# A decode kernel on one core: the last 96 rows of w_out loaded into 24 lanes by transfers of six lanes, new ring places for the last unit's keys, halves in the last projection and in the final copy

## The chip, the cores and the metric

The kernel runs on one core of one Trainium2 chip. The metric is the device time of one execution in microseconds (us), of which the median over several runs is compared. The core has five engines with instruction streams of their own: TensorE (PE, matrix products; its weight loads are listed as PEld), VectorE (DVE), ScalarE (ACT), GpSimd (POOL) and SyncE (SP), and 16 DMA engines that move data between device memory and the on-chip memory of 128 lanes (partitions). Matmul results go to PSUM.

## The reference

One decode step for 4 sequences of one token, D = 640: `out = x + attention(ln(x)) + gmlp(ln(x))`. Cut to what matters:

```python
q = (xn @ wq).reshape(4, 1, 32, 128).transpose(0, 2, 1, 3)
p = softmax(einsum('bhqd,bhkd->bhqk', q, k_cache) * 128 ** -0.5)   # 4 x 32 heads, 4096 keys each
o = einsum('bhqk,bhkd->bhqd', p, v_cache)
attention = o.reshape(4, 1, 4096) @ wo                             # wo: 4096 x 640
z = gelu(xn @ w_in)                                                # w_in: 640 x 1728
z1, z2 = z[..., :864], layernorm(z[..., 864:])
g = w_sp * z2 + b_sp                                               # one token: w_sp is 1 x 1
gmlp = (z1 * g) @ w_out                                            # w_out: 864 x 640
```

Everything is bfloat16; the key and value caches are 134 MB each and are read once.

## The kernel before, in words

Work is cut into 16 units (`NU`): four groups of eight heads times four sequences. A unit's keys are 8 MB and its values 8 MB. Keys lie in a ring of seven places of 2 MB each (`RING`), four places to a unit; values lie in one buffer, `v_all`. `k_at[u]` says which places a unit's four quarters take, `k_order[u]` in which order they are worked on. Even units take places 3 to 6, odd ones 0 to 3; the last three units have entries of their own. Place 4 also takes a group's rows of wo (`WO_AT`), and places 0 to 3 the last unit's values (`VE_AT`), for which `v_all` comes too late.

The main loop goes over 64 steps `n`, one quarter of a unit's keys each. In a step DVE multiplies the quarter by the query in place (`product`, L490), adds the two halves of each row (`fold_half`, L496), PE adds up the rest by eight matmuls with the identity (`sums`, L505), and DVE finishes the row sums one step later (`row_sums`, L518). At a unit's first step the scores of the unit before become weights (`head_max`, `exps`, `by_head`); a few steps later `weighted` (L575) multiplies them with the values. `turns` says at which step that happens. After a group's last unit, `group_turn` and `group_proj` (L636) multiply by wo and add into `out_ps`, the PSUM tile in which all parts of the output are summed: columns 0 to 319 on partitions 0 to 3, columns 320 to 639 on partitions 32 to 35.

The gMLP is a generator, `gmlp`, whose stages are run in steps 0 to 2. It cuts the 864 rows of w_out in `NFF` = 6 blocks of 128 and one of `FT` = 96. For each block and each half of w_in there are five weight loads and matmuls of four columns (L358), then small DVE and ACT steps on tiles with `NFC` = 7 blocks (L366 to L450), and at the end two matmuls for each block into `out_ps` (L454). The weights wq, w_in and the last 96 rows of w_out (`w_end_sb`, one row to a lane) lie in `v_all` until then; so unit 0's values can be loaded only behind the gMLP.

All large loads are issued by SP, in the order of the list `loads`. `pump` goes through the list at each step and stops at the first entry whose places are still `busy`; in the engine's own stream each transfer then waits for what it really needs. The last entries are two halves of unit 15's values (the second in four pieces of 64, 32, 16 and 16 columns of 256 bytes a lane) and the last group's wo in five transfers: heads 0-1, 2-3, 4-5, 6 and 7. The end of the kernel is those heads' matmuls, one copy of `out_ps` by ACT (L758) and two stores, one from ACT's queue and one from SP's.

Of the kernel before, what the change touches and what calls it, by code (L numbers as in the profile page):

```python
# [17 lines left out]
def kernel(  # L18
# [14 lines left out]
    nc = tc.nc  # L33
    P = nc.NUM_PARTITIONS
    Bsz, Sq, D = A_x.shape
    _, H, S, Dh = A_k_cache.shape
    HD = A_wq.shape[1]
    F = B_w_in.shape[1]
    Fh = F // 2
    DC = D // P  # L40
# [8 lines left out]
    HT = 8  # L49
# [3 lines left out]
    NU = HG * Bsz  # L53
# [6 lines left out]
    QW = HC * Dh  # L60
    RING = 2 * NK - 1
    NFF = Fh // P
    NFC = NFF + 1
    FT = Fh - NFF * P
    NOH = D // 2
    CB = 4
    NG = NR // CB
# [25 lines left out]
    v_all = places.tile([P, NK * QW], BF16, name="v_all")  # L93
# [3 lines left out]
    w_in_sb = v_all[:, DC * HD : DC * (HD + F)].rearrange("p (c n) -> p c n", c=DC)  # L97
    w_out_sb = p_m[:].rearrange("p n g c h -> p (n g c h)")[:, 0 : NFF * D].rearrange(
        "p (k n) -> p k n", k=NFF
    )  # L100
    w_end_sb = v_all[:, DC * (HD + F) : DC * (HD + F) + D]
    nc.sync.dma_start(out=wq_sb, in_=A_wq.rearrange("(p c) n -> p c n", c=DC))

    wsp_bf = const.tile([1, 1], BF16)
# [4 lines left out]
    def load_w():  # L109
        nc.sync.dma_start(out=w_in_sb, in_=B_w_in.rearrange("(p c) n -> p c n", c=DC))  # L110
        nc.sync.dma_start(
            out=w_out_sb, in_=B_w_out[0 : NFF * P].rearrange("(p k) n -> p k n", k=NFF)
        )
        nc.sync.dma_start(out=w_end_sb[:FT], in_=B_w_out[NFF * P : Fh])

    def run_of(cache, u):
        hg, b = divmod(u, Bsz)
# [8 lines left out]
    k_at, k_order = {}, {}  # L126
    for u in range(NU):
        k_at[u] = [r if u % 2 else NK - 1 + r for r in range(NK)]
        k_order[u] = [NK - 1, 0, 1, 2] if u % 2 else [0, 1, 2, 3]
    k_order[NU - 3] = [0, 1, 2, 3]  # L130
    k_at[NU - 2], k_order[NU - 2] = [5, 6, 0, 1], [0, 1, 2, 3]
    k_at[NU - 1], k_order[NU - 1] = [2, 3, 5, 6], [0, 1, 2, 3]
    VE_AT, WO_AT = (0, 2), 4

    def k_load(u, r0=0, r1=NK):
        at = k_at[u][r0:r1]

        def go():
            nc.sync.dma_start(
                out=ring[:, at[0] : at[0] + r1 - r0, :],  # L140
                in_=run_of(A_k_cache, u)[:, r0 * QW : r1 * QW].rearrange("p (r w) -> p r w", w=QW),
            )

        return go, at
# [22 lines left out]
    def wo_load(hg):  # L167
        return (lambda: load_wo(hg)), [WO_AT]

    loads = [k_load(0, 0, 2), (load_w, []), k_load(0, 2, 4), k_load(1)]  # L170
    for u in range(NU - 4):
        loads += [v_load(u), k_load(u + 2)]
        if u % Bsz == Bsz - 1:
# [24 lines left out]
    def load_wo(hg):  # L198
        rows = A_wo[hg * HT * Dh : (hg + 1) * HT * Dh]
        if hg == HG - 1:  # L200
            by_head = rows.rearrange("(h p) n -> p h n", p=P)
            for h0, h1 in ((0, 2), (2, 4), (4, 6), (6, 7), (7, 8)):
                nc.sync.dma_start(out=wo_sb[:, h0:h1, :], in_=by_head[:, h0:h1, :])
            return
        nc.sync.dma_start(
            out=wo_sb.rearrange("p (e j) n -> p e j n", e=PAR),
            in_=rows.rearrange("(e p j) n -> p e j n", e=PAR, j=JR),
        )
# [7 lines left out]
    for e in range(PAR):  # L216
        nc.gpsimd.tensor_copy(
            out=of_row[:, e, :, :, e, :],
# [131 lines left out]
    def gmlp():  # L350
        zz, gw, gt, gz = (gm[n] for n in ("zz", "gw", "gt", "gz"))
        zT = ps_pv.tile([P, 2, NFC, Bsz], FP32, tag="pv", name="zT")
        for t in range(2):
            f1 = t * Fh + NFF * P
            w_t = w_in_sb[:, :, t * Fh : f1].rearrange("p c (f k) -> p c k f", k=NFF)
            for k in range(NFC):
                for c in range(DC):
                    nc.tensor.matmul(  # L358
                        out=zT[: P if k < NFF else FT, t, k, :],
                        lhsT=w_t[:, c, k, :] if k < NFF else w_in_sb[:, c, f1 : f1 + FT],  # L360
                        rhs=xnT[:, c, 0:Bsz],
                        start=(c == 0),
                        stop=(c == DC - 1),
                    )
        yield
        nc.vector.tensor_copy(out=zz[:, :, 0:NFF, :], in_=zT[:, :, 0:NFF, :])  # L366
        nc.vector.tensor_copy(out=zz[:FT, :, NFF, :], in_=zT[:FT, :, NFF, :])
        nc.vector.tensor_tensor(out=gw[:], in0=zz[:], in1=zz[:], op=ALU.mult)
        nc.vector.tensor_scalar(
            out=gw[:], in0=gw[:], scalar1=0.044715, scalar2=1.0, op0=ALU.mult, op1=ALU.add  # L370
        )
        nc.vector.tensor_tensor(out=gw[:], in0=gw[:], in1=zz[:], op=ALU.mult)
        nc.scalar.activation(
            out=gt[:], in_=gw[:], func=ACT.Tanh, scale=math.sqrt(2.0 / math.pi)
        )
        yield
        nc.vector.tensor_scalar(
            out=gt[:], in0=gt[:], scalar1=1.0, scalar2=0.5, op0=ALU.add, op1=ALU.mult
        )
        nc.vector.tensor_tensor(out=gz[:, 0:2], in0=zz[:], in1=gt[:], op=ALU.mult)  # L380
        sq = gz[:, 2, :, :]
        nc.vector.tensor_tensor(out=sq, in0=gz[:, 1, :, :], in1=gz[:, 1, :, :], op=ALU.mult)

        s_ps = ps_m.tile([1, 2, NFC, Bsz], FP32, tag="m", name="ln_ps")
        nc.tensor.matmul(
            out=s_ps[:], lhsT=ones_sq[:, 0:1], rhs=gz[:, 1:3], start=True, stop=True
        )
        yield
        st, ac = gm["st"], gm["ac"]
        mean_t = st[:, 0:Bsz]  # L390
        ex2_t = st[:, Bsz : 2 * Bsz]
        var_t = st[:, 2 * Bsz : 3 * Bsz]
        rst_t = st[:, 3 * Bsz : 4 * Bsz]
        tmp_t = st[:, 4 * Bsz : 5 * Bsz]
        nc.vector.tensor_reduce(
            out=st[:, 0 : 2 * Bsz].rearrange("o (s b) -> o s b", s=2),
            in_=s_ps[:].rearrange("o s k b -> o s b k"),
            axis=AX.X,
            op=ALU.add,
        )  # L400
        nc.vector.tensor_scalar(
            out=st[:, 0 : 2 * Bsz],
            in0=st[:, 0 : 2 * Bsz],
            scalar1=1.0 / float(Fh),
            scalar2=None,
            op0=ALU.mult,
        )
        nc.vector.tensor_tensor(out=tmp_t, in0=mean_t, in1=mean_t, op=ALU.mult)
        nc.vector.tensor_tensor(out=var_t, in0=ex2_t, in1=tmp_t, op=ALU.subtract)
        nc.scalar.activation(  # L410
            out=rst_t, in_=var_t, func=ACT.Sqrt, bias=eps_tile[:1], scale=1.0
        )
        wsp_t = work.tile([1, 1], FP32, name="wsp_t")
        nc.vector.tensor_copy(out=wsp_t[:], in_=wsp_bf[:])
        bsp_t = work.tile([1, 1], FP32, name="bsp_t")
        nc.vector.tensor_copy(out=bsp_t[:], in_=bsp_bf[:])
        yield
        nc.vector.reciprocal(out=rst_t, in_=rst_t)
        nc.vector.tensor_scalar(
            out=ac[:, 0:Bsz], in0=rst_t, scalar1=wsp_t[:, 0:1], scalar2=None, op0=ALU.mult  # L420
        )
        nc.vector.tensor_tensor(out=tmp_t, in0=ac[:, 0:Bsz], in1=mean_t, op=ALU.mult)
        nc.vector.tensor_scalar(
            out=ac[:, Bsz : 2 * Bsz],
            in0=tmp_t,
            scalar1=-1.0,
            scalar2=bsp_t[:, 0:1],
            op0=ALU.mult,
            op1=ALU.add,
        )  # L430
        ac_ps = ps_m.tile([P, 2 * Bsz], FP32, tag="m", name="ac_ps")
        nc.tensor.matmul(
            out=ac_ps[:], lhsT=ones_sq[0:1, :], rhs=ac[:], start=True, stop=True
        )
        ac_sb = work.tile([P, 2 * Bsz], FP32, name="ac_sb")
        nc.scalar.copy(out=ac_sb[:], in_=ac_ps[:])
        yield
        nc.vector.tensor_tensor(
            out=sq,
            in0=gz[:, 1, :, :],  # L440
            in1=ac_sb[:, None, 0:Bsz].to_broadcast([P, NFC, Bsz]),
            op=ALU.mult,
        )
        nc.vector.tensor_tensor(
            out=sq,
            in0=sq,
            in1=ac_sb[:, None, Bsz : 2 * Bsz].to_broadcast([P, NFC, Bsz]),
            op=ALU.add,
        )
        nc.vector.tensor_tensor(out=gm["yT"][:], in0=gz[:, 0, :, :], in1=sq, op=ALU.mult)  # L450
        for k in range(NFC):
            w = P if k < NFF else FT
            for half in range(2):
                nc.tensor.matmul(  # L454
                    out=out_sum(half),
                    lhsT=gm["yT"][:w, k, :],
                    rhs=(w_out_sb[:, k] if k < NFF else w_end_sb[:FT])[
                        :, half * NOH : (half + 1) * NOH
                    ],
                    start=False,  # L460
                    stop=False,
                )
        yield
# [206 lines left out]
    with tc.manual_schedule(engines={E.PE, E.DVE, E.Activation, E.SP}):  # L670
# [84 lines left out]

        res = work.tile([P, NOH], BF16, name="res")
        out_v = out.flatten_outer_dims()
        nc.scalar.copy(out=res[0 : OG + Bsz], in_=out_ps[0 : OG + Bsz])  # L758
        nc.scalar.dma_start(out=out_v[:, 0:NOH], in_=res[0:Bsz])
        nc.sync.dma_start(out=out_v[:, NOH:D], in_=res[OG : OG + Bsz])  # L760

# [29 lines left out]
```

## Time and profile before

| | before |
|---|---|
| median of 3 runs | 662.24 us (662.23 to 663.67) |
| the profiled execution: time, span | 662.98 us, 661.2 us |
| mean granted TensorE clock | 0.687 |
| busy: PE, DVE, ACT | 305.8 us, 522.3 us, 29.8 us |
| DMA: moved, mean rate | 282.54 MB, 427 GB/s |
| q1 (loads from SP), share of 16 engines' span | 99.0% |
| first keys landed, first `product` | 25.9 us, 26.02 us |
| unit 0's values issued | 56.08 us |
| unit 15's first keys issued | 572.2 us |
| last wo transfer issued, landed | 649.6 us, 657.8 us |
| final copy, first store | 658.35 us (0.42 us long), 658.8 us |

The profile is one execution, taken by the hardware profiler. "Span" is the time from its first to its last instruction; the execution's own time has 1.78 us more around it. A row of the timeline gives start, duration, engine, line, operation, output and inputs; in brackets stands how long the engine was idle before and what it waited for. SPq is SP's queue: an entry there is the issue of a transfer, not the transfer.

### The profile page before, as it was taken

The page shows a single profiled execution, that of the slowest core. Times are in us where ns is not written, and L with a number is a line of the kernel's source. Part 1 is how long each engine was busy: PE and PEld are TensorE (multiplying, and loading weights), DVE is VectorE, ACT ScalarE, POOL GpSimd, SP SyncE. Part 2 cuts the span into 40 slices and gives each one's busy share as a digit, 9 for nine tenths or more (in the row PEclk, how much of TensorE's full clock was granted, in tenths as well). Part 3 has the DMA queues.
Part 4 walks back from the last instruction along what each step waited for, and adds up shares of the span by engine and source line. Part 5 has one row for each costly group of instructions (what it writes and reads, how often), then busy time and mean ns, then how long its engine had stood idle before and what let it go on. Part 6 is the DMA issues. An engine that isn't in the chain of part 4 may idle for free.

```text
span 661.2 us, 4618 instructions
## 1 busy us (share of the span) xinstructions
PE 305.8 (46%) x1999; PEld 133.8 (20%) x1999; DVE 522.3 (79%) x325; ACT 29.8 (5%) x73; POOL 2.6 (0%) x12
## 2 busy tenths in 40 slices
PE   0265363526427452362536336263462544737357
PEld 0032121212103221120222212121120221213124
DVE  2578977959598794969959697695969969999950
ACT  0020000000000000000000000000000000000000
POOL 1000000000000000000000000000000000000000
PEclk9666586765857676685867878666685867876575
DMA  9999999999999999999999999999999999999996
GB/s 377 424 459 408 437 441 440 433 444 428 413 444 436 441 424 428 441 428 440 437 437 421 425 444 437 432 432 437 424 437 444 428 430 427 413 437 425 460 399 277
DMA packets 8272, 282.54 MB, mean 427 GB/s; under 512 B 848, under 2 KB 1980, under 8 KB 3132
## 3 DMA queue, kind: packets, MB, share of 16 engines
q1 hardware_dynamic: 8232, 282.24, 99.0%
q8 instruction: 15, 0.25, 0.1%
q14 instruction: 5, 0.04, 0.0%
q10 hardware_dynamic: 20, 0.01, 0.0%
HBM read 282.24 MB, written 0.01 MB: 427 GB/s over the span
## 4 chain that ended last, share of the span: by engine, by line
DMA 64%; DVE 26%; PE 9%; issue 1%; ACT 0%; SPq 0%; DVEq 0%
DMA k_ring<-in_A_k_cache_dram 57%; DVE k_ring L490 14%; PE s_ps L505 7%; DVE k_ring L496 7%; DMA v_all<-in_A_v_cache_dram 4%; DMA k_ring<-in_A_wo_dram 3%; DVE s_sb L518 2%; DVE m L527 1%; PE pv L575 1%; DVE p_m L551 1%; PE out_ps L636 1%; DVE mt L529 0%; DVE mt L532 0%; DVE nm L534 0%; DVE o_n L618 0%
## 5 line engine op out<-in xcount | busy, mean ns | idle before, releaser
L490 DVE TENSOR_TENSOR k_ring<-k_ring,qbc 128x8192 bf16<-128x8192 bf16 x64 | 282.8, 4419 | 91.6 <-DMA k_ring<-in_A_k_cache_dram 91.6
L505 PE MATMUL s_ps<-k_ring,ident 128*128 128x512 bf16 x512 | 199.2, 559 | 320.8 <-DVE k_ring L496 320.6
L505 PEld LDWEIGHTS <-ident 128*128 128x128 bf16 x512 | 65.4, 129 | 434.6 <-issue 385.8
L496 DVE TENSOR_TENSOR k_ring<-k_ring 128x4096 bf16<-128x4096 bf16 x64 | 146.1, 2283 | 0.0
L575 PE MATMUL pv<-v_all,p_m 128*32 128x512 bf16 x960 | 59.1, 402 | 0.2 <-DMA v_all<-in_A_v_cache_dram 0.2
L518 DVE TENSOR_REDUCE s_sb<-s_ps 128x64 f32<-128x512 f32 x64 | 43.9, 685 | 5.0 <-PE s_ps L505 5.0
L551 DVE TENSOR_TENSOR p_m<-p_c,own 128x2048 bf16<-128x2048 bf16 x16 | 36.6, 2285 | 0.7 <-ACT p_c L540 0.7
L575 PEld LDWEIGHTS <-p_m 128*32 128x32 bf16 x992 | 26.0, 103 | 39.8 <-issue 15.1
L540 ACT ACTIVATE p_c<-s_sb,nm 128x256 bf16<-128x256 f32 x16 | 8.1, 508 | 334.6 <-DVE nm L534 334.6
L606 PEld LDWEIGHTS o_ps<-o_rows,pick 128*128 128x128 f32 x96 | 19.5, 281 | 3.9 <-issue 2.8
L606 PE MATMUL o_ps<-o_rows,pick 128*128 128x128 f32 x96 | 18.7, 360 | 0.0
L587 ACT COPY o_rows<-pv 128x512 f32<-128x512 f32 x16 | 9.4, 586 | 166.7 <-PE pv L575 166.7
L281 DVE TENSOR_SCALAR q_rows<-q_ps 128x512 bf16<-128x512 f32 x2 | 1.4, 692 | 13.6 <-PE q_ps L273 13.6
L752 DVE TENSOR_TENSOR o_n_last<-o_last,rden_all 128x32 bf16<-128x32 f32 x1 | 0.2, 192 | 13.3 <-PE o_last L744 13.3
L480 ACT CAST qbc<-qbc_ps 128x128 bf16<-128x128 f32 x16 | 4.3, 267 | 104.7 <-PE qbc_ps L472 104.7
L273 PE MATMUL q_ps<-v_all,xnT 128*32 128x512 bf16 x40 | 3.7, 539 | 11.1 <-DMA v_all<-in_A_wq_dram 11.1
L527 DVE TENSOR_REDUCE m<-s_sb 128x1 f32<-128x256 f32 x16 | 6.7, 420 | 0.6
L472 PE MATMUL qbc_ps<-q_rows,of_row 128*128 128x128 bf16 x32 | 5.8, 271 | 0.6 <-DVE q_rows L281 0.6
L472 PEld LDWEIGHTS <-of_row 128*128 128x128 bf16 x32 | 4.1, 132 | 7.9 <-issue 7.3
L653 PE MATMUL o_last<-hot,o_rows 128*128 128x8 f32 x32 | 4.9, 279 | 0.7 <-ACT o_rows L587 0.7
L653 PEld LDWEIGHTS o_last<-hot,o_rows 128*128 128x128 f32 x32 | 4.8, 226 | 1.8 <-ACT o_rows L587 1.7
L575 PE MATMUL pv<-k_ring,p_m 128*32 128x512 bf16 x32 | 3.6, 631 | 2.4 <-DMA k_ring<-in_A_v_cache_dram 2.4
(87 smaller groups left out, 69.0 us busy)
## 6 DMA issues: line engine op xcount, KB each, us to landing
k_ring<-in_A_k_cache_dram SPq DMA_DIRECT2D x6, 4096.0 KB, 20.1
v_all<-in_A_v_cache_dram SPq DMA_DIRECT2D x2, 4096.0 KB, 22.3
v_all<-in_A_wq_dram SPq DMA_DIRECT2D x1, 5120.0 KB, 15.5
k_ring<-in_A_v_cache_dram SPq DMA_DIRECT2D x1, 4096.0 KB, 35.5
k_ring<-in_A_wo_dram SPq DMA_DIRECT2D x3, 1280.0 KB, 20.4
v_all<-in_B_w_in_dram SPq DMA_DIRECT2D x1, 2160.0 KB, 29.4
k_ring<-in_A_v_cache_dram SPq DMA_DIRECT2D x1, 2048.0 KB, 38.8
k_ring<-in_A_v_cache_dram SPq DMA_DIRECT2D x1, 1024.0 KB
```

Of the source, the lines that this page charges most:

```text
L472: nc.tensor.matmul(out=qb_ps[:], lhsT=of_row[:, e, b].rearrange("p k f l -> p (k f l)"), rhs=q_rows[e][:, hg, :], start=(e == 0), stop=(e ...
L490: nc.vector.tensor_tensor(out=t, in0=t, in1=qbcs[u][:, None, :].to_broadcast([P, HC, Dh]), op=ALU.mult)
L496: nc.vector.tensor_tensor(out=t[:, :, 0:HD2], in0=t[:, :, 0:HD2], in1=t[:, :, HD2:Dh], op=ALU.add)
L505: nc.tensor.matmul(out=s[:], lhsT=ident[:], rhs=t[:, :, g * RW : (g + 1) * RW], start=(g == 0), stop=(g == m - 1),)
L518: nc.vector.tensor_reduce(out=scores[u][:, r * HC : (r + 1) * HC], in_=sums_ps.pop(n)[:], axis=AX.X, op=ALU.add,)
L527: nc.vector.tensor_reduce(out=m1[:], in_=scores[u][:], axis=AX.X, op=ALU.max)
L540: nc.scalar.activation(out=p_c[u][:], in_=scores.pop(u)[:], func=ACT.Exp, bias=maxes.pop(u)[:], scale=1.0, accum_out=row_den[hg % NACC][:, ...
L551: nc.vector.tensor_tensor(out=p_m[:, u % 2], in0=p_c.pop(u)[:].rearrange("p (g c) -> p g c", c=CB)[:, :, :, None].to_broadcast([P, NG, CB, HT]
L575: nc.tensor.matmul(out=pvs[u][cg * QD : (cg + 1) * QD, :], lhsT=p_m[:, u % 2, g0 + n].rearrange("p c h -> p (c h)"), rhs=v_at[:, n * CB : ...
L587: nc.scalar.copy(out=o[:].rearrange("p c d -> p (c d)"), in_=pvs.pop(u)[:])
L606: nc.tensor.matmul(out=gr[hg][:], lhsT=pick[:, c, Bsz - 1 - b : P + Bsz - 1 - b], rhs=o[:, c, :], start=(b == 0 and c == 0), stop=(b == Bs ...
L653: nc.tensor.matmul(out=o_last[0][:, :, :, u % Bsz], lhsT=o[:, c, :], rhs=hot[:, c, :].rearrange("p (e k) -> p k e", e=PAR), start=(c == 0) ...
```

## The change

The last 96 rows of w_out are loaded as 24 lanes with four rows each, by four transfers that take every fourth lane (six lanes, 5120 bytes each), behind the second part of unit 0's keys. The gMLP's blocks become six of 128 and four of 24. Unit 13 works on its quarters in the order 0, 1, 3, 2, and unit 15's keys lie in places 3, 4, 5, 6. The last head's rows of wo come as two column halves. The final copy is made half by DVE, half by ACT.

```diff
-    NFC = NFF + 1
-    FT = Fh - NFF * P
+    FR = 4
+    FT = (Fh - NFF * P) // FR
+    NFC = NFF + FR
+    LS = 4
...
-    w_end_sb = v_all[:, DC * (HD + F) : DC * (HD + F) + D]
+    end_at = -(-DC * (HD + F) // 256) * 256
+    w_end_sb = v_all[:, end_at : end_at + FR * D].rearrange("p (r n) -> p r n", r=FR)
...
-        nc.sync.dma_start(out=w_end_sb[:FT], in_=B_w_out[NFF * P : Fh])
+    def load_w_end():
+        rows = B_w_out[NFF * P : Fh].rearrange("(p r) n -> p r n", r=FR)
+        for l in range(LS):
+            nc.sync.dma_start(out=w_end_sb[l:FT:LS], in_=rows[l:FT:LS])
...
-    k_order[NU - 3] = [0, 1, 2, 3]
+    k_order[NU - 3] = [0, 1, 3, 2]
     k_at[NU - 2], k_order[NU - 2] = [5, 6, 0, 1], [0, 1, 2, 3]
-    k_at[NU - 1], k_order[NU - 1] = [2, 3, 5, 6], [0, 1, 2, 3]
+    k_at[NU - 1], k_order[NU - 1] = [3, 4, 5, 6], [0, 1, 2, 3]
...
-    loads = [k_load(0, 0, 2), (load_w, []), k_load(0, 2, 4), k_load(1)]
+    loads = [k_load(0, 0, 2), (load_w, []), k_load(0, 2, 4), (load_w_end, []), k_load(1)]
...
-            for h0, h1 in ((0, 2), (2, 4), (4, 6), (6, 7), (7, 8)):
+            for h0, h1 in ((0, 2), (2, 4), (4, 6), (6, 7)):
                 nc.sync.dma_start(out=wo_sb[:, h0:h1, :], in_=by_head[:, h0:h1, :])
+            for half in range(2):
+                cols = slice(half * NOH, (half + 1) * NOH)
+                nc.sync.dma_start(out=wo_sb[:, HT - 1, cols], in_=by_head[:, HT - 1, cols])
...
                         out=zT[: P if k < NFF else FT, t, k, :],
-                        lhsT=w_t[:, c, k, :] if k < NFF else w_in_sb[:, c, f1 : f1 + FT],
+                        lhsT=w_t[:, c, k, :]
+                        if k < NFF
+                        else w_in_sb[:, c, f1 + k - NFF : f1 + FT * FR : FR],
...
-        nc.vector.tensor_copy(out=zz[:FT, :, NFF, :], in_=zT[:FT, :, NFF, :])
+        nc.vector.tensor_copy(out=zz[:FT, :, NFF:], in_=zT[:FT, :, NFF:])
...
-                    rhs=(w_out_sb[:, k] if k < NFF else w_end_sb[:FT])[
+                    rhs=(w_out_sb[:, k] if k < NFF else w_end_sb[:FT, k - NFF])[
...
-        nc.scalar.copy(out=res[0 : OG + Bsz], in_=out_ps[0 : OG + Bsz])
+        mid = NOH // 2
+        nc.vector.tensor_copy(out=res[0 : OG + Bsz, 0:mid], in_=out_ps[0 : OG + Bsz, 0:mid])
+        nc.scalar.copy(out=res[0 : OG + Bsz, mid:NOH], in_=out_ps[0 : OG + Bsz, mid:NOH])
```

## The prediction

> **What bounds the kernel now.** I read the page first: engines, slices, DMA queues.
>
> ```profile
> span 661.2 us, 4618 instructions
> ...
> DVE  2578977959598794969959697695969969999950
> ...
> DMA  9999999999999999999999999999999999999996
> ...
> q1 hardware_dynamic: 8232, 282.24, 99.0%
> q8 instruction: 15, 0.25, 0.1%
> ```
>
> The 16 DMA engines never rest until the last slice; VectorE (DVE) is busiest of the rest and has gaps. 282.24 MB sets the length. Next, the chain of waits for the end (start, length, what), and the first and last steps in the timeline:
>
> ```profile
> 608.76 26.27 DMA v_all<-in_A_v_cache_dram
> 635.03 0.02 issue
> 635.05 21.96 DMA k_ring<-in_A_wo_dram
> 657.01 0.04 issue
> 657.06 1.27 PE out_ps L636 x8
> 658.33 0.02 issue
> 658.35 0.42 ACT res L758
> ```
>
> ```profile
> 36.21 3.32 PEld L358 LDWEIGHTS <-v_all 128*128 128x128 bf16 x70
> ...
> 39.73 0.21 DVE L366 COPY zz<-zT 128x48 f32<-128x48 f32 x1 [2.62 <-PE zT L358]
> ...
> 54.02 1.76 PE L454 MATMUL out_ps<-p_m,yT 128*4 128x320 bf16 x12 [2.67 <-DVE yT L450]
> ...
> 56.08 0.33 SPq L150 DMA_DIRECT2D v_all<-in_A_v_cache_dram  x1
> ```
>
> The end hangs on the last wo transfer, then four heads' matmuls, a copy, the store. "v_all 56.08" is unit 0's V load, which the gMLP (second list) holds back.
>
> Then the trace's single DMA packets (queue, start, duration, bytes). A 32,768-byte packet takes 1213 ns in steady state on every engine, and each packet starts where one ended, so 16 chains can be followed. Three things show. (1) The 15 packets of q8 hold 16,384 bytes each; each stops one chain for 0.88 to 1.06 us, and the order of the chains repeats after eight (40.8 and 404.7 stop one chain, 88.7 and 446.6 the next, 274.5 and 639.6 the last engine's): eight engines are stopped about twice, the others are not. (2) So a transfer's 16 parts land apart: unit 13's keys between 531.37 and 535.28, the last wo piece at 655.24 to 655.79 on eight engines, at 656.73 to 657.26 on seven, and at 657.84 on one, which is last on every load from unit 14's V on. That one engine ends the kernel. (3) It never runs dry: the time from a load's issue plus 1.1 us (unit 15's first keys, issued 572.23, started at 573.2 to 573.4 on engines already empty) to that engine's end of the load before is at least 3.2 us everywhere; for unit 0's V it is 5.6.
>
> **The change, part by part.** I sum against the profiled execution: 662.98 us, its span 661.2 and 1.78 around it; the median of the runs is 662.24, 0.74 lower, and I apply the difference to the median.
>
> *Rows of w_out.* Before, 96 partitions of 1280 bytes: six packets on each of 16 engines, and the last engine landed them 0.31 us after the load before (33.68, 33.99). After, four transfers of six lanes, 5120 bytes each. The x transfer of four partitions left four data packets on four chains, that of one partition one packet, so I take one packet per lane: six engines get four packets, ten get none. Bytes are the same; per engine the six go from 0.31 to 4 x 0.20 = 0.80 us (5120 bytes at 27.0 bytes/ns is 0.19, with its completion write 0.20), +0.48, and the ten lose 0.31. If the last engine is one of the ten, the end moves by -0.31. Is it? I take it that transfers of few lanes begin at the same engine, so that the six hold the one of one-lane transfers. That one I know: the two-byte packets of w_sp and b_sp stop one chain, and up to 573 it is never hit by q8 and is ahead. A second, by its start a lane of x, isn't hit either. So the eight that are hit look like a block apart from the six. I take -0.31, nearest to these rows; the other end is +0.48. The Trainium skill, page "DMA: Bandwidth & Descriptors", section "Why a DMA increments its semaphore by 16 and not by 1", says that the largest number up to 16 that divides the partitions is used, on the lowest-numbered engines; the x rows agree with the count. The same page's "Rules for kernel authors" speaks against the change: make the outer size a multiple of 16, and join transfers under 64 KB. By that rule six engines end the load and the sum would carry the +0.48, the first rival.
>
> *Their issue.* Three more DMAs on SyncE (SP). The trace shows that every DMA reuses one of eight completion semaphores and waits for the transfer eight before it. The second new transfer waits for wq (landed 16.27), and SP with it; the load behind, unit 1's keys, could not go before 36.35 anyway (it waits for the ring place), and its own semaphore is now that of the first keys (25.92). The rows land with or just behind unit 0's second keys (44.0), and are read after 54. Zero; without that cover it would be SP's lateness, beyond 6 us of slack.
>
> *gMLP.* 30 more weight-load and matmul pairs: 70 take 3.32 us, so 30 take 1.42, and DVE already waits 2.62 there, so all of it lands on DVE. Eleven small DVE steps widen from 56 or 28 to 80 or 40 columns, 1.04 ns each (48 columns 0.21 us, 512 columns 0.69): 0.2. Six more projections: matmuls of the two output halves start together in the trace, a pair every 0.267 us, so 0.80. Unit 0's V is issued 2.4 us later, 58.5; 5.6 of slack for the last engine, 4.0 for the first. DVE waits for the next keys anyway and catches up. Zero. 72 more TensorE (PE) instructions move the q8 packets a few us earlier; a sixteenth would hit the chain next in turn, which started 0.8 us ahead of the last engine: zero.
>
> *Places and order.* Unit 15's first keys need places 3 and 4 instead of 2 and 3; with unit 13's order 0, 1, 3, 2 they can go about 7 us earlier (565 instead of 572.2). Place 4 is free since the group projection (549). That fills a hole of 0.1 to 0.5 us on the engines that are ahead; the last engine had 3.2 us left. The later V pieces go up to 11 us earlier, wo 1.3 us earlier, all behind a full queue. Zero for the end.
>
> *Last wo head as halves.* Eight packets of 1280 bytes take 52 ns apart, 0.42 us. Sixteen of 640: at the same rate the same; the stores' 640-byte packets took 29 to 39 ns, so +0.05 to +0.20. I take +0.06, near the short ones. The gain would be a matmul done earlier, but the two matmuls of the last head start at 657.880 and 657.884 and take 0.43 together: nothing is saved, at most 0.1. The sixth wo transfer waits for the second piece of the last V (652.04, before 649.60 for the fifth); 1.1 us of latency and 1.2 of a full queue (the fifth's issue took 1.17) leave 2 us before 656.9. Zero.
>
> *Split copy.* ScalarE (ACT) takes 0.17 for 8 columns, 0.27 for 128, 0.42 for 320: 0.29 for 160. DVE by its line above 0.33. The store waits for the later one: -0.09. If the two halves were made one after the other, 0.62, +0.20; if DVE is as quick as ACT, -0.13.
>
> Sum: -0.31 + 0.06 + 0 - 0.09 = **-0.34**: span 660.86, median 662.24 - 0.34 = **661.9**.
>
> **Rivals.**
> 1. *The six are late engines* (chance 0.15). If the last engine is one of them: +0.48 + 0.06 - 0.09, 662.7. If the second (657.26) is, it ends at 657.74, 0.10 before the old end: 662.1. For: I can name only two of sixteen chains. Against: both are ahead.
> 2. *The tail edits cost instead of saving* (0.08): slow halves +0.20, copies in a row +0.20, with the relief -0.31: 662.3. Against: the trace's waits are per region (V pieces wait for single places).
> 3. *The added PE work holds unit 0's V so long that the queue dries* (0.04): slower. It decides from 5.6 us of lateness on the last engine. If narrow weights did not overlap, 30 x (0.185 + 0.143, the group means) is 9.8, plus 6 x 0.47 and 0.2: 12.8, so 7.2 lost: 669.4. Against: ten 96-wide ones already run in the 3.32 us stream.
> 4. *The rows don't go where the change says* (0.04): if a six-lane transfer is cut to use all 16 engines, no engine is relieved, and -0.03 is left: 662.2. Against: the x packets, one per lane.
>
> My forecast has 0.66; 0.03 is left for a gain that no row here shows.
>
> **Numbers.** About what a measurement of this kernel can tell from no change is 0.3%, 2 us: 660.25 to 664.2. The forecast and rivals 1, 2 and 4 lie inside; rival 3 is outside, slower. Runs of before spread by 1.4 (662.23 to 663.67), so 0.02 more goes to slower: faster 0.03, same 0.91, slower 0.06. The range: low, -0.31 - 0.13 and 0.1 for a matmul, 661.7, less 0.6 for the spread of runs: 661.1; high, rival 1's 662.7 with 0.4 for it: 663.1.
>
> **What would show it.** Right: four loads of 30 KB of w_out, the second issued just after 16.3; unit 0's V issued near 58.5 and no gap in the last engine's packets; unit 15's keys near 565; the last wo landing near 657.6 with the last engine closer to the second; last matmul still 0.43; copies of 0.29 and 0.33 side by side. Wrong: the last landing after 657.9 (six late engines), two copies in a row, V of unit 0 after 61.5, or the DMA share of q1 clearly under 99.0%.

## The result, and the profile after

| | before | after |
|---|---|---|
| median, runs side by side | 662.86 us (662.23 to 668.87, 9 runs) | 668.55 us (668.12 to 668.94, 9 runs) |
| ratio after / before | | 1.0077, 95% interval 1.0056 to 1.0098 |
| the profiled execution: time, span | 662.98 us, 661.2 us | 668.77 us, 667.0 us |
| unit 0's values issued | 56.08 us | 65.11 us |
| unit 15's first keys issued | 572.2 us | 570.5 us |
| last wo transfer landed | 657.84 us | 663.35 us |
| copying of `out_ps` | 0.42 us | 0.63 us |

The changed kernel is slower by 5.7 us, where 0.3 us less was predicted, and outside the range. Again the page first.

```profile
span 667.0 us, 4696 instructions
...
DVE  2539897959689594987969599595968959999950
...
DMA  9997899999999999999999999999999999999996
...
q1 hardware_dynamic: 8312, 282.24, 98.3%
q8 instruction: 16, 0.26, 0.1%
```

The bytes are the same. In the DMA row the fourth and fifth slices (50 to 83 us), which were 9 and 9, are 7 and 8. The share of q1 puts a size on it: 99.0% of 661.2 is 654.6 us of transfers and 6.6 us without; 98.3% of 667.0 is 655.7 and 11.3. So 4.7 us of the 5.8 are time in which the engines had nothing to do, and about 1.1 (the shares are rounded to 0.1%, or 0.7 us) is transfer time. The table by stretches places the idle time. It gives the stretch, its length, the busy time of PE, PEld, DVE, ACT and POOL with the number of instructions in brackets, PE's granted clock, and last the DMA engines' mean busy share and GB/s. A share can come out slightly over 1, so only differences are read. First before, then after:

```profile
60.00:70.00 10.00, 2.76 (x8) 0.97 (x8) 9.02 (x9) 0.45 (x2) 0.00 (x0) 0.67 0.98 426
```

```profile
60.00:70.00 10.00, 6.45 (x28) 2.16 (x29) 7.73 (x7) 0.73 (x1) 0.00 (x0) 0.50 0.56 216
```

From 0.98 to 0.56 of ten microseconds is 4.2 us, on the average of 16 engines. Added up from the single packets, cut at the edges of the stretch, the idle time is 4.98 us in after and nothing in before. The first packets behind the hole are slow as well: the 16 of 64 KB took 3.00 us on average, where 2.42 is usual in both runs. By the packets, all sixteen finished unit 1's keys between 60.7 and 62.6 and began unit 0's values between 66.07 and 67.11. The timelines say why (start, length, what; in brackets the wait before it). Before:

```profile
36.27 3.35 PE L358 MATMUL zT<-xnT,v_all 128*128 128x4 bf16 x70
```

After:

```profile
30.78 2.97 SPq L122 DMA_DIRECT2D v_all<-in_B_w_out_dram  x4
...
36.05 0.35 SPq L147 DMA_DIRECT2D k_ring<-in_A_k_cache_dram  x1
...
43.27 4.21 PE L369 MATMUL zT<-xnT,v_all 128*128 128x4 bf16 x100 [7.15 <-DMA v_all<-in_B_w_out_dram]
...
47.59 0.21 DVE L379 COPY zz<-zT 128x48 f32<-128x48 f32 x1 [10.84 <-PE zT L369]
...
62.16 1.76 PE L467 MATMUL out_ps<-p_m,yT 128*4 128x320 bf16 x12 [2.92 <-DVE yT L463]
...
65.11 0.33 SPq L158 DMA_DIRECT2D v_all<-in_A_v_cache_dram  x1
```

The gMLP's first matmuls read w_in, which landed at 30.7; before, they began at 36.27. Now they begin at 43.27, after 7.15 us of waiting for a load of w_out: the four transfers of the last 96 rows, which landed between 42.4 and 43.0, behind unit 0's second keys. They don't read these rows, nor any column that these transfers write. All that follows is late by these 7 us, by 0.9 for the longer run of matmuls, and by 1.2 in the steps behind; unit 0's values go 9.03 us later. The issue of the four transfers is odd as well. The waits of SP's queue give it (what is waited for: us in all, times, longest):

```profile
SPq L122 <- DMA v_all<-in_B_w_in_dram: 27.0, 1, 27.0
```

The first of them waits for w_in to land, though it writes other columns. So a writer that came after w_in, and a reader of w_in, are both ordered against transfers that share no byte with them. Two things set these four transfers apart from every other large load of the kernel: they go to six lanes only, and they step over lanes by four, `l:FT:LS`. The theory is that the step does it; the experiments test this.

At the end the chain of waits shows the two parts of the split copy in a row, not side by side:

```profile
640.52 21.93 DMA k_ring<-in_A_wo_dram
662.49 1.34 PE out_ps L649 x8
663.85 0.33 DVE res L772
664.20 0.28 ACT res L773
```

### The profile page after: what moved, and what is told of

Same layout as the page of the kernel before. It is cut to its first block, busy times and chain, and to the rows that moved or that the text cites. A ratio compares the mean times of both kernels' runs of the same rounds, so it can differ in the third digit from the quotient of the medians.

```text
span 667.0 us, 4696 instructions
## 1 busy us (share of the span) xinstructions
PE 308.9 (46%) x2035; PEld 132.8 (20%) x2035; DVE 522.7 (78%) x326; ACT 29.7 (4%) x73; POOL 2.7 (0%) x12
## 3 DMA queue, kind: packets, MB, share of 16 engines
q1 hardware_dynamic: 8312, 282.24, 98.3%
## 4 chain that ended last, share of the span: by engine, by line
DMA 66%; DVE 22%; PE 10%; issue 1%; SPq 0%; DVEq 0%; ACT 0%
DMA k_ring<-in_A_k_cache_dram 48%; DVE k_ring L503 11%; DMA v_all<-in_A_v_cache_dram 9%; PE s_ps L518 7%; DVE k_ring L509 6%; DMA v_all<-in_B_w_in_dram 4%; DMA k_ring<-in_A_wo_dram 3%; DVE s_sb L531 2%; DMA v_all<-in_B_w_out_dram 1%; PE pv L588 1%; DVE m L540 1%; PE out_ps L649 1%; PE zT L369 1%; PE out_ps L467 0%; DVE mt L542 0%
## 5 line engine op out<-in xcount | busy, mean ns | idle before, releaser
L619 PEld LDWEIGHTS o_ps<-o_rows,pick 128*128 128x128 f32 x96 | 18.1, 262 | 4.0 <-issue 3.0
L619 PE MATMUL o_ps<-o_rows,pick 128*128 128x128 f32 x96 | 17.0, 335 | 0.0
L369 PE MATMUL zT<-xnT,v_all 128*128 128x4 bf16 (+1 forms) x100 | 4.2, 178 | 7.1 <-DMA v_all<-in_B_w_out_dram 7.1
L369 PEld LDWEIGHTS <-v_all 128*128 128x128 bf16 (+1 forms) x100 | 4.1, 126 | 7.3 <-DMA v_all<-in_B_w_out_dram 7.3
```

Source lines behind the costliest of these rows:

```text
L369: nc.tensor.matmul(out=zT[: P if k < NFF else FT, t, k, :], lhsT=w_t[:, c, k, :] if k < NFF else w_in_sb[:, c, f1 + k - NFF : f1 + FT * FR ...
L619: nc.tensor.matmul(out=gr[hg][:], lhsT=pick[:, c, Bsz - 1 - b : P + Bsz - 1 - b], rhs=o[:, c, :], start=(b == 0 and c == 0), stop=(b == Bs ...
```

## The experiments

Three theories. **W**: the lane-stepped transfers make the gMLP wait, unit 0's values are late, the queue runs dry. **P**: the added PE work or the four transfers' own packets cost the time (the prediction's rivals 3 and 1). **R**: the rest of the change does. The times of before in these batches were 662.65, 662.60, 662.51 and 662.52 (15 to 34 runs each).

**e1, the changed kernel with neighbouring lanes.** One thing is different from after: each of the four transfers takes six lanes that lie next to each other.

```diff
         for l in range(LS):
-            nc.sync.dma_start(out=w_end_sb[l:FT:LS], in_=rows[l:FT:LS])
+            s = slice(l * FT // LS, (l + 1) * FT // LS)
+            nc.sync.dma_start(out=w_end_sb[s], in_=rows[s])
```

> The changed kernel, but each of the four transfers takes six neighbouring lanes (0-5, 6-11, ...) instead of every fourth lane; all else as changed. Theory W (a transfer that steps over lanes makes the gMLP's first matmuls wait for it, and it itself waits for w_in): both waits go, unit 0's V is issued near 58.5 us instead of 65.1, the DMA engines don't run dry, 661.9 us (my old forecast, +-0.4). Theory P (the added matmuls and wider steps delay V): nothing changes, V at 65, 668.5. Theory R (places, halves and split copy cost the time): 668.5, with V at 58.5.

Measured: 663.29 us (663.12 to 667.03), ratio to before 1.000 (0.9979 to 1.0021); after's interval, 1.0056 to 1.0098, doesn't touch it. The loss is gone, though the time is 1.4 over the 661.9 that was expected. The timeline of e1, and its stretch from 60 to 70 us:

```profile
36.04 4.22 PE L370 MATMUL zT<-xnT,v_all 128*128 128x4 bf16 x100
...
57.89 0.35 SPq L159 DMA_DIRECT2D v_all<-in_A_v_cache_dram  x1
```

```profile
60.00:70.00 10.00, 4.67 (x12) 1.42 (x11) 8.73 (x8) 0.00 (x0) 0.00 (x0) 0.80 0.97 419
```

The same 100 matmuls take the same 4.2 us, but begin at 36.04 with no wait, and the hole is gone. So 5.26 us of the change come with the step in the lanes (5.05 if each run is taken against before in its own batch), and the added PE work (all of it is still in e1) isn't what holds unit 0's values.

**e2, only the rows of w_out** (as in the change, stepped, with the gMLP's blocks of 24), **and e3, only the rest** (places, order, halves, split copy).

> The kernel before with the change of the w_out rows alone (24 lanes, four transfers that step over lanes, behind unit 0's second keys); places, wo and copy as before. W and P: the whole loss is here, V at 65.1, 668.5 us (+-0.4). R: 662.2.

> The kernel before with the other three parts alone (unit 13's order and unit 15's places, last wo head as column halves, split copy); the rows of w_out as before. W and P: -0.09 for the copy and +0.06 for the halves, within 0.3 of the kernel before. R: 668.

Measured: e2 668.44 us, ratio 1.0076 (1.0053 to 1.0098), values of unit 0 at 64.89; e3 662.76 us, ratio 0.9981 (0.9958 to 1.0004), values at 55.69. The whole loss is in the rows; R falls.

**e4, the wait alone, and f1, its control.** Before is left as it is; behind unit 0's second keys four more transfers bring the same rows once more, to columns of `v_all` that nothing reads. In e4 they step over the lanes by four, in f1 they take neighbours.

```diff
+    def load_again():
+        at = 117 * 256
+        again = v_all[:, at : at + 4 * D]
+        rows = B_w_out[NFF * P : Fh].rearrange("(p r) n -> p (r n)", r=4)
+        for l in range(4):
+            nc.sync.dma_start(out=again[l : FT // 4 : 4], in_=rows[l : FT // 4 : 4])   # e4
+            nc.sync.dma_start(out=again[6 * l : 6 * l + 6], in_=rows[6 * l : 6 * l + 6])   # f1
...
-    loads = [k_load(0, 0, 2), (load_w, []), k_load(0, 2, 4), k_load(1)]
+    loads = [k_load(0, 0, 2), (load_w, []), k_load(0, 2, 4), (load_again, []), k_load(1)]
```

> The kernel before, and behind unit 0's second keys four more transfers like the changed kernel's (six lanes, every fourth, 5120 bytes), into a stretch of the V buffer that nobody reads; no added matmuls. W: the gMLP's first matmuls wait for them (43 to 44.8 us instead of 36.3), V is issued 6.7 to 8 us later, 63 to 64, the engines run dry for 1 to 4 us: 664 to 667 us. P: V at 56, 662.3.

> The control of the run before it: the kernel before with the same four unread transfers of six lanes behind unit 0's second keys, but of neighbouring lanes instead of every fourth. W: nobody waits for them, the gMLP's matmuls start at 36.3 and V is issued at 56 us; the time is that of the kernel before, 662.7 us, or up to 0.8 more if the engine that ends last is one of the six that carry them (4 x 0.196 us). P and a theory that the six-lane traffic itself costs the time: 667, as with every fourth lane.

Measured: e4 667.45 us (666.7 to 668.89), ratio 1.0059 (1.0039 to 1.0079); f1 663.71 us (663.27 to 666.76), ratio 1.0011 (0.9994 to 1.0029). Both are a little over the top of what was expected, 667 and 663.5. Timeline of e4:

```profile
43.66 3.72 PE L365 MATMUL zT<-xnT,v_all 128*128 128x4 bf16 x70 [7.19 <-DMA v_all<-in_B_w_out_dram]
...
63.85 0.34 SPq L157 DMA_DIRECT2D v_all<-in_A_v_cache_dram  x1
```

and of f1:

```profile
36.24 3.37 PE L365 MATMUL zT<-xnT,v_all 128*128 128x4 bf16 x70
...
56.08 0.35 SPq L157 DMA_DIRECT2D v_all<-in_A_v_cache_dram  x1
```

The 70 matmuls of before, with their old operands, wait 7.19 us for data that nobody uses, as soon as the transfers step over lanes. This is W by itself, without any of the added work. The DMA share from 60 to 70 us is 0.57 in e4 and 1.00 in f1. In e4 the four transfers were issued from 16.14 on, not held up by w_in, and the matmuls wait as long as in after; so the late issue in after is no part of that wait.

**f4, the stepped transfers ahead of unit 0's second keys**, otherwise the changed kernel: the matmuls still have to wait for them, but they land early.

```diff
-    loads = [k_load(0, 0, 2), (load_w, []), k_load(0, 2, 4), (load_w_end, []), k_load(1)]
+    loads = [k_load(0, 0, 2), (load_w, []), (load_w_end, []), k_load(0, 2, 4), k_load(1)]
```

> The changed kernel with its four transfers (every fourth lane) in front of unit 0's second keys instead of behind them. W in numbers: the first of them waits for w_in (30.7 us), SP issues the four until 33.8 and unit 0's second keys only then, so the engines, done with w_out at 32.5, stand for about 2 us; the gMLP's matmuls wait for a landing near 35 only, less than DVE's own wait, and V goes at 58 to 59 without a hole. So the loss moves to another place and shrinks: 664.5 to 666 us. P: 668.5 or more.

Measured: 666.39 us (666.13 to 666.55, 6 runs), ratio 1.0052 (1.0034 to 1.007). Its timeline and its stretch from 16 to 60 us:

```profile
30.83 2.97 SPq L122 DMA_DIRECT2D v_all<-in_B_w_out_dram  x4
33.85 2.68 SPq L147 DMA_DIRECT2D k_ring<-in_A_k_cache_dram  x2
36.17 4.22 PE L369 MATMUL zT<-xnT,v_all 128*128 128x4 bf16 x100
```

```profile
16.00:60.00 44.00, 21.21 (x187) 10.26 (x187) 30.06 (x32) 5.11 (x8) 0.00 (x0) 0.91 0.95 403
```

The gMLP is on time (its values go at 58.92), so the late hole is gone; but now the wait for w_in in SP's queue holds back unit 0's second keys, to 33.85, and the queue runs dry there: the share is 0.95 where e1 has 1.03. By the single packets the engines stand still for 2.65 us, and the time is 3.1 over e1's, a little more than was expected. Each of the two waits costs where it meets something that is due.

**f2, the rows alone in neighbouring lanes, and f3, the places and the order alone.**

> The kernel before with the w_out rows in 24 lanes alone, by transfers of six neighbouring lanes; places, wo and copy as before. W: V at 58, no hole in the transfers. Then the balance of the engines is left: 662.3 us if the last engine is one of the ten that lose 0.31, 663.1 if it is one of the six (+0.48). P: 668.

> The kernel before with unit 13's order and unit 15's places alone. My forecast: no difference, 662.6 us +-0.2, unit 15's first keys issued near 565 instead of 572. If the earlier issue gained anything it would be at most the hole of 0.5 on the engines ahead. The rest of the three other parts (halves, copy) is then the difference to their joint run, 662.76; its profile shows the two copies one after the other, so +0.1 to +0.3 is expected from them.

Measured: f2 663.04 us (662.85 to 663.29), ratio 0.9998 (0.9983 to 1.0013); f3 662.45 us (662.14 to 667.25), ratio 1.0001 (0.9984 to 1.0018), with unit 15's first keys at 564.47. The places do what was forecast and bring nothing. The rows, without the wait, cost 0.44 by the medians where -0.31 had been taken; e1 less e3 gives 0.53. Intervals of this width can't decide on half a microsecond, but the two differences agree, and 22 of before's 30 runs are under the lowest of f2. Three more runs ask where it comes from.

**g2, the PE work alone**: before with 36 more pairs of weight load and matmul in zT, whose results nothing reads. **g3, the load alone**: the rows by four transfers of six neighbouring lanes, the PE work of before. **h1**: as g3, but every transfer goes to 32 lanes. In g3 and h1 the products of the last 96 rows are made with rows that lie elsewhere, so their outputs lack these rows; and as nothing reads `v_all` that late, unit 0's values go at 43.60 and 44.87 instead of 56.08, which the expectations below do not reckon with.

```diff
-        again = v_all[:, at : at + 4 * D]                  # g3
-        rows = B_w_out[NFF * P : Fh].rearrange("(p r) n -> p (r n)", r=4)
-        for l in range(4):
-            nc.sync.dma_start(out=again[6 * l : 6 * l + 6], in_=rows[6 * l : 6 * l + 6])
+        again = v_all[:, at : at + 3 * D]                  # h1
+        rows = B_w_out[NFF * P : Fh].rearrange("(p r) n -> p (r n)", r=3)
+        for l in range(4):
+            cols = slice(l * 3 * D // 4, (l + 1) * 3 * D // 4)
+            nc.sync.dma_start(out=again[:32, cols], in_=rows[:, cols])
```

> The kernel before with 36 more pairs of weight load and matmul in zT, whose results nothing reads; every load as before. Theory Q (the rows in blocks of lanes cost 0.44 because the 72 added PE instructions bring the q8 packets earlier, so that more engines have been stopped twice at the end, another engine among them the last): a sixteenth q8 packet before 657, the last wo piece lands some 0.4 us later than before, 663.0. Rival D (it is the four transfers' own packets): 662.6, last landing near 657.8 or earlier.

> The kernel before without the 96-lane load: four transfers of six neighbouring lanes bring the same bytes, and the last 96 rows' products are made with rows that are already there, so the output lacks them; as many PE instructions as before. Theory Q: the ten engines lose 0.31, the six gain 0.48, q8 as before: the last landing at 657.5 to 657.9, 662.3 to 662.6. Rival D: the six engines end the load, the last landing near 658.3, 663.0.

> As g3 (the 96-lane load gone, the same bytes brought by four transfers, the products made with rows that are already there, so the output lacks the last 96 rows), but each transfer has 32 lanes of 960 bytes instead of six lanes of 5120. Theory D (the six lanes' packets make six engines late, and the end goes by one of them): every engine gets eight packets of some 0.04 us, about 0.35 in all where before has 0.31, so the time is that of before, 662.4 to 662.7, and g3's +0.55 is gone. Rival O (it is the four transfers themselves, or their place behind unit 0's second keys, whatever the lanes): 663.0 to 663.1.

Measured: g2 662.52 us (662.27 to 673.94), 0.01 over before; g3 663.06 us (662.52 to 663.24), 0.55 over; h1 662.83 us (662.57 to 663.22), 0.31 over. g2's page has the sixteenth q8 packet:

```profile
q8 instruction: 16, 0.26, 0.1%
```

It started at 655.8, and yet the last wo piece landed at 657.76, as before: theory Q falls, and more PE instructions cost nothing. That leaves the load. By the packets, 14 of g3's 24 packets of 5120 bytes took 196 ns and the other ten 231 to 393: 0.93 us on each of six engines, where before has 0.34 on each of sixteen. h1's 128 packets of 960 bytes took 44 ns, eight to an engine, 0.35. Spreading the load took 0.23 back by the medians, about half, though intervals of this width can't decide on that either; the other 0.3 is neither D nor Q as they were put. The packets behind the load changed too. The first 64 KB packet of unit 1's keys on each engine takes up to 2.83 us in g3 and up to 2.96 in h1, where before has 2.42. That is 0.39 and 0.45 us on the average of 16 engines, against 0.20 for the packets behind the 96-lane load in before (0.12 to 0.26 in e3, f3 and g2, which keep that load). With the load's own packets it is 0.54 us an engine in before, 0.73 in g3 and 0.80 in h1. This could be most of h1's 0.31; no run shows that it is. Why packets behind the four transfers are slow stays open, and so does the effect of the earlier values in g3 and h1, and which engine ended last: the profiled run of g3 landed its last piece at 657.79, that of before (itself 0.5 above its median) at 657.84.

**g1, a result tile for each engine**, on f3: DVE's half and ACT's half of the final copy go to tiles of their own, by four stores.

```diff
-        res = work.tile([P, NOH], BF16, name="res")
...
-        nc.scalar.copy(out=res[0 : OG + Bsz], in_=out_ps[0 : OG + Bsz])
+        left = work.tile([P, mid], BF16, name="res_l")
+        right = work.tile([P, mid], BF16, name="res_r")
+        nc.vector.tensor_copy(out=left[0 : OG + Bsz], in_=out_ps[0 : OG + Bsz, 0:mid])
+        nc.scalar.copy(out=right[0 : OG + Bsz], in_=out_ps[0 : OG + Bsz, mid:NOH])
```

> The kernel before with the new places, and the final copy split over two result tiles, one for each engine, stored by four DMAs (two on SP, two on ACT). Theory T (in the changed kernel ACT waits for DVE because both write one tile): the two copies, 0.32 and 0.28 us, begin within 0.1 us of each other, and copying ends 0.3 us earlier than in a row; against 0.42 for one copy, 0.1 is saved, less what two more stores cost: 662.1 to 662.6. Rival U (the wait is for the PSUM bank that both read): the copies stay in a row, 0.63 us, and the time is 662.7 or more.

Measured: 662.82 us (662.58 to 669.1), ratio 0.9999 (0.9968 to 1.003). The profiled execution is one of 667.44 us, so only order and durations at its end are read:

```profile
662.47 0.32 DVE L760 CAST res_l<-out_ps 36x160 bf16<-36x160 f32 x1 [2.97 <-PE out_ps L636]
...
662.82 0.28 ACT L761 CAST res_r<-out_ps 36x160 bf16<-36x160 f32 x1 [9.63 <-DVE res_l L760]
```

ACT still waits for DVE, though it shares no tile with it but the one that both read, `out_ps`. Theory T falls. The instruction's own wait is on DVE; in before the copy waits on PE. That leaves the PSUM tile which both read, though no run gave each copy a PSUM tile of its own. The Trainium skill, page "PSUM — Partial Sum Buffer", section "PSUM bank collisions raise a hardware error", says that two engines must not be in the same bank and quarter of the lanes at once, not even both reading, and that the compiler puts such accesses in a row. The trace agrees: here they are in a row.

No version beats the kernel before by more than the runs can tell: f3, the places alone, is the nearest (662.45 against 662.60).

## Why the prediction was wrong, by its own steps

- **"Their issue", priced at zero: the step that failed; it cost 5.3 us.** It asked what is queued on SP behind the new transfers, and that part held: unit 1's keys went at 36.05 (36.35 before). It took the time of first use from what the code reads ("are read after 54") and so never asked who else is made to wait for the landing. The matmuls of w_in were, from 36.27 to 43.27. "The rows land with or just behind unit 0's second keys" was right, and is exactly why the wait is 7 us long (7.15 before the first matmul, and unit 0's values 9.03 us later, where 2.4 had been forecast). The issue just after 16.3 that it expected is seen in e1 (15.92) and f1 (16.30), not in after (30.78).
- **Rival 3 had the right mechanism and the wrong trigger.** The queue does dry up behind late values of unit 0, at 60 to 67 us. But narrow weights are cheap: 100 pairs take 4.21 us, 0.86 more than the 70 of before, under the 1.42 of the sum and far from the rival's 9.8; e1 and f2 issue the values at 57.89 and 58.37 (58.5 forecast) and show no hole. Also its way from lateness to loss was off. The lateness of unit 0's values against the 56.08 of before, the idle time from 60 to 70 us by the packets, and the loss are 7.77, 3.10 and 3.74 in e4 (loss against f1), 9.03, 4.98 and 5.26 in after (against e1), 8.81, 4.74 and 5.40 in e2 (against f2). The idle time is an average of 16 engines, and lateness less idle time is 4.1 to 4.7, between the slacks that the prediction had named for the first engine, 4.0, and the last, 5.6; it let the last decide. The loss is 0.3 to 0.7 more than the idle time, and the slow first packets behind the hole, 0.6 us an engine, are of that size.
- **"Rows of w_out", -0.31: wrong sign.** +0.44 to +0.55 by medians (f2, e1 less e3, g3), the size of the other end, +0.48, and of rival 1. The sum counted the load's own packets at 0.20 us each and took those behind it as unchanged; in g3 the six engines needed 0.93 us instead of 0.80, and the packets behind were slower on nearly all engines, by 0.39 us on average. f1, which adds the four transfers and removes nothing, stands 1.1 over before, with 1.0 us more on six engines and 0.38 on average behind them. That the last engine is one of the six isn't shown: h1, on all engines, keeps 0.31. The rule of the Trainium skill that the prediction set against the change (page "DMA: Bandwidth & Descriptors", "Rules for kernel authors": few, large transfers, outer size a multiple of 16) pointed the right way, for half a microsecond.
- **"Split copy", -0.09: wrong sign.** 0.32 and 0.28 were forecast well (0.33 and 0.29), but not side by side: 663.85 to 664.48 is 0.63 against 0.42, the +0.20 that rival 2 gave for "copies in a row". "The trace's waits are per region" was the argument against it; it came from `k_ring`, and this wait is between two readers of a PSUM tile. e3 less f3, which holds halves and copy, is 0.31 (0.26 with each against before in its own batch).
- **Right:** "Places and order", zero, with the keys at 564.5 (565 forecast); "gMLP", zero for the PE work (g2: 0.01, with a sixteenth q8 packet that cost nothing); the halves of the last head, no gain: the copy starts 0.51 us after the last landing with halves (e3, 657.50 to 658.01) and without (f3, 657.29 to 657.80).

Put together: 5.3 for the wait, 0.5 for the rows' load and 0.2 for the copy make 6.0; measured are 5.7 to 5.9 (668.55 against 662.86 in the same runs, 662.65 in the next). All four signs that the prediction named for its being wrong came: the last landing after 657.9 (663.35, because of the hole and not of six late engines), the copies in a row, unit 0's values after 61.5 and q1 clearly under 99.0%. It gave no thought to a way in which the last two could come with cheap PE work.

## What to carry to other kernels

Find out when data is used from the instructions' waits, not from what the code reads: an unusual form of access, such as the step over lanes here, can be ordered against neighbours in the same buffer that it doesn't touch. Where a buffer is shared by several loads, load each in neighbouring lanes, and look after each edit for a new wait on the first reader of every other part. And price a late load by the time that the engines stand still on average, not by the slack of the one that ends last: in these runs the loss was that average and 0.3 to 0.7 us more.

## What the runs showed of the hardware and the program that was not expected

- Transfers that step by four lanes of `v_all` order themselves behind the load of w_in (27.0 us of SP's queue in after) and hold the matmuls that read w_in (7.15 us; 7.19 in e4). In e4 the second happens without the first. Which rule of the program's ordering makes this so, no run shows; a tile of its own for the rows would tell, and there was no room for one.
- The issue of a stepped transfer took longer: four took 2.97 us on SP in after, three neighbouring ones 0.95 in e1.
- The first 64 KB packets behind a hole in the queue took 3.00 us on average (after), and those behind four small transfers up to 2.96 us (h1), where 2.42 us is usual. No run shows why.
- Two engines that read different columns of one PSUM tile were put in a row (g1: 0.03 us from the end of DVE's copy to the start of ACT's).
